# Weight sums of the second projection, made in the first layer and kept in DRAM, with another order of small steps in its blocks

## The chip, the cores and the metric

The kernel runs on one core of a Trainium2 chip. The core has five engines that each follow their own list of instructions: PE (TensorE, matrix products), DVE (VectorE), ACT (ScalarE), POOL (GpSimd) and SP (SyncE, which only issues DMAs here). An engine works through its list in order, and an instruction whose semaphore wait is not met holds up everything behind it on that engine. POOL issues DMAs too, out of the same list as its arithmetic.

The metric is the device time of one execution in microseconds, lower being better. Before the change it was 1901.19 us, the median of three runs (1899.56 to 1901.35).

## The reference, cut to what matters

Two layers, each an attention block and a gated block, all on x of 2048 rows by 448 features. The weights are the same in both layers.

```python
def _A_ref(x, wqkv, wo):              # D = 448, 16 heads of 28
    qkv = (x @ wqkv).reshape(B, S, 3, H, Dh) ...
    p = _softmax(einsum(q, k) * Dh ** -0.5)
    return (p @ v) @ wo
def _B_ref(x, w_gate, w_up, w_down):  # F = 1792
    return (_sigmoid(x @ w_gate) * (x @ w_up)) @ w_down
x = A_x
x = x + _A_ref(_layernorm(x), ...)
x = x + _B_ref(_layernorm(x), ...)
x = x + _A_ref(_layernorm(x), ...)
x = x + _B_ref(_layernorm(x), ...)
```

## The kernel before, in words

The rows of x are worked in four blocks of 512 (`b0` to `b3`), and x stays in SBUF. The program is a straight list: no scheduler moves anything, so the order of the calls in the Python source is the order on each engine. Small steps are threaded into the larger ones by hand, through lists of functions (`fill`, `points`, `between`).

**First layer's projection** (start to about 118 us). For each block, `qk` makes seven 128-column tiles of Q and K on PE (`qkp`, L618). ACT copies a tile out as float16 (L865), DVE makes the remainder (L866, the "low" part), ACT squares (L868) and DVE takes maxima (L872) that PE sums into `qnorm` and `knorm` (L844, L847), three tiles late. `vals` makes V (`vp`, L643 to L645), which ACT copies out (L1114). A block's normalised rows come from `norm` (DVE statistics; POOL `rs`, L333 and L335), `squares` (DVE scaling L362 and 32x32 transposes L379 into a tile `xs`), `store` (four DMAs of SP, `xs` to the DRAM tile `xt_scr`, L391) and `gather` (SP reads `xt_scr` back, L399 and L401). Beside it `Measure.read` loads weights whose sizes are wanted later; the rows of gate and up weights are loaded by POOL (six DMAs, L215 and L218, tile `raw`).

**The test of the bounds.** During the V of the third block DVE writes `guard`, `worst` and `flag` (L1216 to L1225). Every engine then loads `flag` into a register (L1231) and branches (L1232) over a part that is needed only for loose bounds. In the program this stands behind two of the four V products of the last block, and the other two stand behind the place where the branches meet.

**The gated block** ends with a tail: the last products with the down weights (`dnp`, L1875) in pieces, whose banks DVE adds into x (L1893). Down weights come by POOL's queue (`dn`, L1769). Beside the tail the second layer's projection is prepared: `add_pair(0)`, `(1)` and `(2)` make the sums of pairs of Q/K weight tiles from the raw weights, which POOL loads (`read_pairs`, L728 to L731): four additions on DVE (L254), four high parts on ACT (L263), six low parts on DVE (L266), and for the third pair two scalings ahead (L747). `load_rest` loads what is left of the weights (six DMAs of SP, L760 to L763). Block 2 of x is normalised there too: statistics, POOL's `rs` and `off` (L333 to L346), `lift` on ACT (L350), transposes (L358).

**Second layer's projection** (about 957 to 1061 us). `qk_sums` works blocks 0, 2 and 3 with the weight sums, by seven products of halves in place of eight: `chain` and `side` products (L633), whose results ACT and DVE add (L962, L978) into tiles `one` and `two`; a single tile `alone` (L1004) has no partner. `points`, `fill` and the list `before` say where steps of other blocks stand among these.

SBUF tiles come from 19 equal slots. `put` returns a slot to the end of the free list, `put_next` to its front, so that the next `get` takes it; a tile in a reused slot waits until everything that used the slot is done.

Of the kernel before, what the change touches and what calls it, by code (L numbers as in the profile page):

```python
# [121 lines left out]
def interleaved_layers(ctx: ExitStack, tc: tile.TileContext, x_in, wqkv, wo, w_gate, w_up,  # L122
# [181 lines left out]
    class Block:  # L304
# [79 lines left out]
        def store(self, queues=(nc.sync,)):  # L384
            xs = self.xs
            uid[0] += 1
            self.scr = dpool.tile([NQ, 32, 4, P], F32, name=f"xt_scr{uid[0]}", tag="xt_scr",
                                  bufs=2)
            for i in range(4):
                r = slice(32 * i, 32 * i + 32)  # L390
                queues[i % len(queues)].dma_start(  # L391
                    self.scr[:, :, i, :].rearrange("j r n -> r j n"),
                    xs[r].rearrange("r j t c -> r j (t c)"))
            big.put(xs)
# [255 lines left out]
    o_parts = dpool.tile([P, 2, 4, D], F16, name="o_parts")  # L650
    gu_parts = dpool.tile([NP, 2, P, N_SUMS, P], F16, name="gu_parts")
    dn_parts = dpool.tile([N_DN, P, NP, 2, DN], F16, name="dn_parts")

    class WeightsQKV:
        def tiles(self):
# [80 lines left out]
        def load(self):  # L736
            self.held, self.sums = [], []

        def add_pair(self, j):
            v, t = self.pair(j), big.get("wsums", [P, 32, P], F16)  # L740
            self.held.append(t)
            self.sums.append(t[:, 0:N_SUMS])
            m = [int(i > ALONE) for i in PAIRS_QK[j]]
            by = up[:, m[0]:m[0] + 1]
            if m[0] != m[1]:
                for z in range(2):
                    nc.vector.tensor_scalar(v[:, :, z], v[:, :, z], up[:, m[z]:m[z] + 1], None,  # L747
                                            op0=ALU.mult)
# [71 lines left out]
    def project(layer, wq, begun):  # L820
# [69 lines left out]
        def qk_sums(b, blk, points, before=None, defer=False):  # L890
# [132 lines left out]
            if before:  # L1023
                before(False)
            pa.c11_c22()
# [6 lines left out]
            pb.c21()  # L1032
            pb.tiles[0].low(pb.one)
            pa.c12()
            pb.c12()
            if before:
                before()
# [12 lines left out]
            pc.third()  # L1050
            at(4)
            pb.tiles[0].square()
            pc.c11_c22()
# [11 lines left out]
            squares = deque([lone.square, pc.tiles[0].square, pc.tiles[1].square])  # L1065
            if not defer:
                squares.popleft()()
            pc.tiles[1].high()
            pc.tiles[1].low(pc.two)
            while squares and not defer:  # L1070
                squares.popleft()()
            at(5)

            def finish(whole=True):
                if not whole:
                    squares.popleft()()
                    return
# [85 lines left out]
        if layer == 0:  # L1163
# [3 lines left out]
                    lambda: b2.ready(0, 1), lambda: (b2.ready(2, 3), b3.store())]  # L1167
            fin = qk(1, b1, fill, None)
            vals(1, b1, {0: b3.gather, 2: fin})
            add = tell.add  # L1170
            fin = qk(2, b2, [idle, lambda: b3.ready(0, 1), lambda: b3.ready(2, 3), idle, add,
                             add, add], None)
            fin = qk(3, blks[3], [add, add, add], fin)
        else:
# [5 lines left out]
            fin = qk_sums(0, blks[0], {0: ready[0:1] + s3[0:1], 1: ready[1:2], 2: s3[1:2],  # L1180
                                       4: ready[2:3], 5: ready[3:4]})
            vals(0, blks[0], {0: both(s3[2], s3[3], s3[6]), 1: both(fin, s3[4], s3[7]),
                              2: both(s3[5], s3[8], s3[9], b3.store),
                              3: both(h2[0], h2[1], b3.gather)})
            fin = qk(1, b1, h2[2:9], None)
            big.put(*wq.qk)
            vals(1, b1, {0: h2[9], 1: both(fin, *h3[0:2]), 2: both(*h3[2:4]),
                         3: both(*h3[4:6])}, banks=(3, 0, 2, 1))
            fin = qk_sums(2, b2, {0: h3[6:7], 1: h3[7:8], 2: h3[8:9], 4: h3[9:10]}, None, True)
# [14 lines left out]

        def guard_of_norms():
# [7 lines left out]
            guard = big.get("guard", [H, S], F16)  # L1213
            zero = big.get("zero", [H, S], F16)
            nc.gpsimd.memset(zero, 0.0)
# [3 lines left out]
            big.put(guard, zero)  # L1219

# [9 lines left out]
        vals(3, blks[3], {}, range(2))  # L1230
# [551 lines left out]
    def gated(layer, first, wt, wq):  # L1782
# [243 lines left out]
        for b, p in seq:  # L2026
# [58 lines left out]
            if b == NB - 1 and not last and p == NP - 2:  # L2085
                wq.read_pairs((0, 1))
# [157 lines left out]
```

## Time and profile before

| | |
|---|---|
| time, median of three runs | 1901.19 us |
| time of the profiled execution | 1900.52 us |
| its span, first instruction to last | 1898.8 us |
| PE busy | 1880.8 us, 99% of the span |
| DVE busy | 1478.7 us, 78% |
| ACT busy | 1425.2 us, 75% |
| POOL busy | 249.2 us, 13% |

A row of a timeline gives the start and the length in us, the engine, the line of the kernel, the operation, the tiles written and read, and in brackets how long the engine was idle ahead of it and what ended that. A row of the waits gives who waited for what, the total, the count and the longest, in us. A row of the windows gives for a stretch of time the busy time and count of each engine, then the clock granted to PE, the busy share of the DMA engines and GB/s.

### The profile page before, as it was taken

The numbers are of one execution on the slowest core, as the hardware profiler recorded it, in microseconds if no ns is written. First come the engines' busy times: TensorE is split into PE (matmuls) and PEld (weight loads), VectorE is DVE, ScalarE is ACT, GpSimd is POOL, SyncE is SP. The second block draws the span as 40 slices with busy tenths as digits, with TensorE's granted clock in tenths as the row PEclk, the third lists the DMA queues.
The fourth block names the chain that finished last, engine by engine and source line by source line (L and its number), as shares of the span: only waits on it lengthen the run. The fifth ranks groups of instructions, "written<-read, shape, count | busy, mean of one in ns | idle before, by whom it ended". The sixth has DMA issues, their size and how long they took to land. (4 is left out here: it accounts for less than half of the span.)

```text
span 1898.8 us, 57166 instructions
## 1 busy us (share of the span) xinstructions
PE 1880.8 (99%) x24531; PEld 1385.4 (73%) x24531; DVE 1478.7 (78%) x2984; ACT 1425.2 (75%) x1885; POOL 249.2 (13%) x482
## 2 busy tenths in 40 slices
PE   9999999999999999999999999999999999999999
PEld 4456656656566899999967556678766768999999
DVE  7758989898977887788876577787787688877664
ACT  5569999999993655555567799999999746555541
POOL 3023112222102111112310000000000021111110
PEclk9999999999999999999999999999999999999999
DMA  7675444344323755646672421222120256566553
GB/s 247 192 216 159 134 131 121 111 121 132 102 87 100 256 206 203 241 183 225 220 192 85 107 51 32 47 52 48 31 52 13 75 159 225 200 228 225 211 207 141
DMA packets 116471, 273.78 MB, mean 144 GB/s; under 512 B 14478, under 2 KB 72590, under 8 KB 116080
## 3 DMA queue, kind: packets, MB, share of 16 engines
q0 software_dynamic: 33120, 163.33, 24.0%
q1 hardware_dynamic: 81936, 105.33, 19.9%
q8 instruction: 194, 3.18, 0.7%
q10 hardware_dynamic: 1152, 1.38, 0.3%
q14 instruction: 69, 0.57, 0.1%
HBM read 210.98 MB, written 50.62 MB: 138 GB/s over the span
## 5 line engine op out<-in xcount | busy, mean ns | idle before, releaser
L1530 ACT ACTIVATE prob_s<-sc 128x1536 f32<-128x1536 f32 (+1 forms) x657 | 888.3, 1478 | 9.6 <-PE sc L1515 8.0
L1566 PE MATMUL acc<-prob_s,val_s 128*32 128x256 f32 (+3 forms) x7700 | 580.3, 384 | 0.9 <-issue 0.9
L1515 PE MATMUL sc<-qp_s 114*32 114x512 f16 x7868 | 562.8, 379 | 0.8 <-DMA qp_s<-g_scr 0.8
L633 PEld LDWEIGHTS <-gu_s 128*128 128x128 f16 x4368 | 426.7, 98 | 46.4 <-PE op L1695 0.7
L1515 PEld LDWEIGHTS <-qp_s 114*32 114x32 f16 x8192 | 293.1, 96 | 186.7 <-issue 72.4
L1566 PEld LDWEIGHTS acc<-prob_s,val_s 128*32 128x32 f32 x7700 | 295.4, 110 | 122.6 <-issue 12.5
L1875 PE MATMUL dnp<-dn_s,hparts_s 128*128 128x224 f16 x2184 | 246.0, 259 | 1.7 <-DVE x L1893 1.7
L633 PE MATMUL chain<-xwide_s,gu_s 128*128 128x256 f16 x2016 | 247.5, 273 | 0.1
L1875 PEld LDWEIGHTS <-hparts_s 128*128 128x128 f16 x2184 | 210.2, 98 | 7.0 <-issue 1.9
L1546 DVE SCALAR_TENSOR_TENSOR power_q<-power_q,expo_q 128x512 f32<-128x512 f32 x243 | 168.2, 692 | 8.3
L1948 ACT COPY one_q<-chain 128x256 f32<-128x256 f32 x224 | 82.4, 372 | 113.2 <-PE chain L633 112.7
L1964 DVE TENSOR_TENSOR one_q<-side,one_q 128x512 f32<-128x512 f32 x112 | 72.1, 686 | 95.7 <-PE side L633 95.4
L633 PE MATMUL side<-xshort_s,gu_s 128*128 128x256 f16 x1120 | 140.6, 273 | 0.0
L1756 POOL DMA_DIRECT2D gu_s<-gu_parts x104 | 56.3, 541 | 428.2 <-PE side L633 426.8
L1595 DVE STREAM_TRANSPOSE oturned_q<-acc 128x512 f32<-128x512 f32 x32 | 22.9, 717 | 98.9 <-PE acc L1566 98.8
L1828 ACT CAST hparts_s<-hsums_q 128x256 f16<-128x256 f32 (+1 forms) x152 | 71.5, 485 | 37.9 <-DVE hsums_q L1840 23.4
L1566 PE MATMUL acc<-power_q,val_s 128*32 128x256 f32 (+3 forms) x300 | 94.2, 396 | 0.0
L633 PE MATMUL side<-xwide_s,gu_s 128*128 128x256 f16 x672 | 91.7, 273 | 0.0
L618 PE MATMUL qkp<-xhl_s,wqk_s 128*128 128x512 f16 x385 | 86.5, 379 | 0.9 <-ACT wqk_s L235 0.6
L1975 ACT ACTIVATE one_q<-one_q 128x512 f32<-128x512 f32 x56 | 35.3, 630 | 64.3 <-DVE one_q L1964 64.0
L1540 DVE TENSOR_SCALAR expo_q<-aside,base 128x512 f32<-128x512 f32 x81 | 60.6, 748 | 22.7 <-PE aside L1515 22.4
L1832 DVE TENSOR_TENSOR hparts_s<-hsums_q,hparts_s 128x256 f16<-128x256 f32 (+1 forms) x152 | 72.7, 520 | 5.8 <-ACT hparts_s L1828 5.8
(261 smaller groups left out, 2396.7 us busy)
## 6 DMA issues: line engine op xcount, KB each, us to landing
gu_s<-gu_parts POOLq DMA_DIRECT2D x104, 800.0 KB, 6.0
dn_s<-dn_parts POOLq DMA_DIRECT2D x42, 784.0 KB, 7.3
qp_s<-qk_scr SPq DMA_DIRECT2D x96, 224.0 KB
gu_parts<-pack_s POOLq DMA_DIRECT2D x14, 800.0 KB, 3.8
xt_scr<-xs_s SPq DMA_DIRECT2D x48, 224.0 KB
xraw_s<-xt_scr SPq DMA_DIRECT2D x12, 768.0 KB
qk_scr<-qkhl_q SPq DMA_DIRECT2D x35, 256.0 KB
qp_s<-qk_scr SPq DMA_DIRECT2D x64, 112.0 KB
```

The lines of the kernel that those rows point to most:

```text
L618: nc.tensor.matmul(pm, w, x, start=(i == 0), stop=(i == len(terms) - 1))
L633: nc.tensor.matmul(pm, a, x, start=(first and i == 0), stop=(i == len(terms) - 1), skip_group_check=True)
L1515: nc.tensor.matmul(ps[32 * j:32 * j + 32, :], hd.k[:, keys], hd.q[:, qb * W:(qb + 1) * W], start=True, stop=True, tile_position=(0, 32 * j))
L1530: nc.scalar.activation(prob[:, 0:n, :], ps[:, 0:n, :], AF.Exp, scale=exp_scale)
L1540: nc.vector.tensor_scalar(y, ps, base2[:, 0:1], -126.0, op0=ALU.mult, op1=ALU.max)
L1546: nc.vector.scalar_tensor_tensor(p, p, c[k], y, op0=ALU.add, op1=ALU.mult)
L1566: nc.tensor.matmul(acc[qb * VC:(qb + 1) * VC, s], v[:, kc % TB, h, :], probs[c * NB + qb][:, s], start=(kc == 0 and a == 0), stop=(kc == N ...
L1828: nc.scalar.copy(to[:, :, 0], a)
L1832: nc.vector.tensor_tensor(to[:, :, 1], a, to[:, :, 0], op=ALU.subtract)
L1875: nc.tensor.matmul(pm, a[:, x, t], w[:, p, y], start=(begin and n == 0 and (j == 0 or alone)), stop=(n == 2), skip_group_check=True)
L1948: nc.scalar.copy(to, pm)
L1964: nc.vector.tensor_tensor(one[m], side[m], one[m], op=ALU.add)
```

## The change

- **Sums kept.** `add_pair` becomes `keep_pair`: the same arithmetic, but it writes a tile `pack`, and POOL stores that to a new DRAM tile `qs_parts` (three pieces of 800 KB). It runs in the first layer's projection: pair 0 in the third block's `qk`, pair 1 behind `guard`, pair 2 at the head of the last block's V. At the end of the first layer's gated block SP loads the three pieces (`wq.load(0)` to `(2)`).
- **The tail of the gated block.** With the three `add_pair` gone, all of block 2's normalisation and its `store` stand at once ahead of the additions into x, two `load_dn` stand there in place of three (the loop issues the rest), and `load_rest` is called there.
- **Order inside `qk_sums`.** The addition of `c11_c22` of the third pair and a square stand ahead of the point 4; the last high and low part of the third pair join the deferred steps; the earlier block's deferred steps are taken up in other places, and its last ones ahead of `pb`'s low part. The half steps of blocks 2 and 3 are spread anew.
- **`store` returns `xs` by `put_next`.** The next `get` takes that slot. In the first layer's projection, for block 2, this is the `raw` tile of the gate and up rows.
- **`zero`** is set ahead of the power that `guard` needs.

```diff
@@ store
-            big.put(xs)
+            big.put_next(xs)
@@ WeightsQKV
-        def add_pair(self, j):
-            v, t = self.pair(j), big.get("wsums", [P, 32, P], F16)
-            self.held.append(t)
-            self.sums.append(t[:, 0:N_SUMS])
+        def keep_pair(self, j):
+            v, t = self.pair(j), big.get("pack", [P, N_SUMS, P], F16)
...
             split_sums(t, v, by)
+            nc.gpsimd.dma_start(qs_parts[j], t)
+            big.put(t)
...
+        def load(self, j):
+            self.held.append(big.get("wsums", [P, 32, P], F16))
+            self.sums.append(self.held[j][:, 0:N_SUMS])
+            nc.sync.dma_start(self.sums[j], qs_parts[j])
@@ qk_sums
             pc.third()
+            pc.c11_c22()
+            pb.tiles[0].square()
             at(4)
-            pb.tiles[0].square()
-            pc.c11_c22()
...
-            squares = deque([lone.square, pc.tiles[0].square, pc.tiles[1].square])
-            if not defer:
-                squares.popleft()()
-            pc.tiles[1].high()
-            pc.tiles[1].low(pc.two)
-            while squares and not defer:
-                squares.popleft()()
+            def last_parts():
+                pc.tiles[1].high()
+                pc.tiles[1].low(pc.two)
+            todo = deque([lone.square, last_parts, pc.tiles[0].square, pc.tiles[1].square])
+            while todo and not defer:
+                todo.popleft()()
@@ project, layer 0
+            fill[4] = lambda: wq.read_pairs((0,))
             fin = qk(1, b1, fill, None)
             vals(1, b1, {0: b3.gather, 2: fin})
-            fin = qk(2, b2, [idle, lambda: b3.ready(0, 1), lambda: b3.ready(2, 3), idle, add,
-                             add, add], None)
+            fin = qk(2, b2, [lambda: wq.keep_pair(0), lambda: b3.ready(0, 1),
+                             lambda: (b3.ready(2, 3), wq.read_pairs((1, 2))), idle, add, add,
+                             add], None)
...
             big.put(guard, zero)
+            if layer == 0:
+                wq.keep_pair(1)
...
-        vals(3, blks[3], {}, range(2))
+        vals(3, blks[3], {} if layer else {0: lambda: wq.keep_pair(2)}, range(2))
@@ gated, the tail
-            wq.load()
-            for _ in range(3):
+            for _ in range(2):
                 wt.load_dn(nc.gpsimd)
-            wq.add_pair(0)
-            wq.add_pair(1)
+            wq.load(1)
+            wq.load(2)
+            wq.load_rest()
             third = after[2]
-            turns = third.squared()
-            between = deque([turns[0:1], [lambda: wq.read_pairs((2,))] + turns[1:2],
-                             turns[2:5] + turns[6:8], turns[5:6] + turns[8:] + [third.store],
-                             [third.gather, lambda: wq.add_pair(2)],
-                             [wq.load_rest, wq.load_values]])
+            for do in third.squared() + [third.store]:
+                do()
+            between = deque([[], [], [third.gather, wq.load_values], [], [], []])
```

Three places show what moves. On POOL, in the first layer's projection, beside the second block's Q and K: the loads of the gate and up rows stand ahead of `rs` of the fourth block. The brackets name the semaphores that a row waits for (DMAHW are the queues that SP and ACT issue into, by number). Before:

```order
41 L215 DMA raw_s_555<-in_B_w_gate_dram 128x3x256 [waits DMAHW1_49,DMAHW2_49,DMAHW0_49,Activation_49]
42 L218 DMA raw_s_555<-in_B_w_gate_dram 64x256 x2
43 L215 DMA raw_s_555<-in_B_w_up_dram 128x3x256
44 L218 DMA raw_s_555<-in_B_w_up_dram 64x256 x2
45 L333 TENSOR_SCALAR rs_607<-mv_606 128x4 [waits DVE_49]
46 L335 TENSOR_TENSOR rs_607<-rs_607,nhalf 128x4 [waits Pool_49]
```

After:

```order
41 L215 DMA raw_s_556<-in_B_w_gate_dram 128x3x256 [waits DMAHW5_49,DMAHW6_49,DMAHW4_49,DMAHW7_49,DMAHW0_49,DVE_49]
42 L218 DMA raw_s_556<-in_B_w_gate_dram 64x256 x2
43 L215 DMA raw_s_556<-in_B_w_up_dram 128x3x256
44 L218 DMA raw_s_556<-in_B_w_up_dram 64x256 x2
45 L333 TENSOR_SCALAR rs_608<-mv_607 128x4 [waits DVE_49]
46 L335 TENSOR_TENSOR rs_608<-rs_608,nhalf 128x4 [waits Pool_49]
47 L732 DMA raws_s_692<-in_A_wqkv_dram 128x3x128 [waits DMASW0_49,Activation_49]
48 L734 DMA raws_s_692<-in_A_wqkv_dram 64x128 [waits DMASW1_49]
```

The order of the rows is the same; the first load now waits for the third block's last transpose (DVE) and its four stores (DMAHW4 to 7), whose slot it takes, and no longer for the use of raw Q/K/V weights on ACT.

On DVE, ahead of the branch of the first layer, before (`guard`, `worst` and `flag`, then the load of the flag):

```order
166 L1210 SCALAR_TENSOR_TENSOR bnd_1126<-top_1125 16x1
167 L1216 TENSOR_SCALAR guard_s_1155<-zero_s_1156,bnd_1126 16x2048
168 L1224 TENSOR_REDUCE worst_1128<-bounds_1200 1x1
169 L1225 TENSOR_SCALAR flag_1127<-worst_1128,back 1x1
170 L1231 TENSOR_LOAD flag_1127
171 L1232 COMPARE_AND_BRANCH
```

After, from the row right behind the one that writes the flag (pair 1's ten rows stand between `guard` and `worst` in the same way):

```order
190 L746 TENSOR_SCALAR raws_s_899<-raws_s_899,up 128x4x128 x2
191 L254 TENSOR_TENSOR sums_q_1275<-raws_s_899 128x256
192 L254 TENSOR_TENSOR sums_q_1275<-sums_q_1275,raws_s_899 128x256
193 L254 TENSOR_TENSOR sums_q_1276<-raws_s_899 128x256
194 L254 TENSOR_TENSOR sums_q_1276<-raws_s_899,sums_q_1275 128x256
195 L266 SCALAR_TENSOR_TENSOR pack_s_1272<-raws_s_899,ones,pack_s_1272 128x256
196 L266 SCALAR_TENSOR_TENSOR pack_s_1272<-sums_q_1275,ones,pack_s_1272 128x512
197 L266 SCALAR_TENSOR_TENSOR pack_s_1272<-sums_q_1276,ones,pack_s_1272 128x384
198 L266 SCALAR_TENSOR_TENSOR pack_s_1272<-raws_s_899,ones,pack_s_1272 128x256
199 L266 SCALAR_TENSOR_TENSOR pack_s_1272<-sums_q_1276,ones,pack_s_1272 64x128
200 L266 SCALAR_TENSOR_TENSOR pack_s_1272<-raws_s_899,ones,pack_s_1272 64x256
201 L1244 TENSOR_LOAD flag_1163
```

Twelve instructions of pair 2 now stand between the writing of the flag and DVE's load of it.

On DVE, in the tail of the first layer's gated block (`hparts` are parts of the hidden values, `x<-dnp` the additions into x, `sums` and `wsums` the weight sums). Before:

```order
2796 L1832 TENSOR_TENSOR hparts_s_13729<-two_q_18251,hparts_s_13729 128x256
2797 L1893 SCALAR_TENSOR_TENSOR x<-dnp_17156,back,x 128x2x224
2798 L254 TENSOR_TENSOR sums_q_18437<-raws_s_18234 128x256
2799 L254 TENSOR_TENSOR sums_q_18437<-sums_q_18437,raws_s_18234 128x256
2800 L254 TENSOR_TENSOR sums_q_18438<-raws_s_18234 128x256
2801 L254 TENSOR_TENSOR sums_q_18438<-raws_s_18234,sums_q_18437 128x256
2802 L266 SCALAR_TENSOR_TENSOR wsums_s_18436<-raws_s_18234,up,wsums_s_18436 128x256
2803 L266 SCALAR_TENSOR_TENSOR wsums_s_18436<-sums_q_18437,up,wsums_s_18436 128x512
```

After:

```order
2830 L330 BN_AGGR mv_18509<-st_0_18511 128x2
2831 L329 BN_STATS st_1_18514<-x 128x6
2832 L330 BN_AGGR mv_18509<-st_1_18514 128x2
2833 L329 BN_STATS st_2_18522<-x 128x6
2834 L330 BN_AGGR mv_18509<-st_2_18522 128x2
2835 L329 BN_STATS st_3_18525<-x 128x6
2836 L330 BN_AGGR mv_18509<-st_3_18525 128x2
2837 L358 STREAM_TRANSPOSE xs_s_18540<-lifted_q_18532 128x14x32
2838 L358 STREAM_TRANSPOSE xs_s_18540<-lifted_q_18534 128x14x32
2839 L358 STREAM_TRANSPOSE xs_s_18540<-lifted_q_18536 128x14x32
2840 L358 STREAM_TRANSPOSE xs_s_18540<-lifted_q_18538 128x14x32
2841 L1906 SCALAR_TENSOR_TENSOR x<-dnp_18550,back,x 128x2x224
```

Ahead of the first addition of the tail stand four statistics and four transposes in place of twenty instructions of two pairs of weight sums.

More of the change, by code (lines that the diff above doesn't have):

```diff
@@ L654, in interleaved_layers, with __init__ @@
     class WeightsQKV:
+        def __init__(self):
+            self.held, self.sums = [], []
         def tiles(self):
@@ L1024, in qk_sums @@
                 before(False)
+                before(False)
             pa.c11_c22()
@@ L1032, in qk_sums @@
             pb.c21()
+            if before:
+                before()
             pb.tiles[0].low(pb.one)
@@ L1203, in project @@
         worst = cpool.tile([1, 1], F32, name=f"worst{layer}", tag="worst", bufs=1)
+        guard = big.get("guard", [H, S], F16)
+        zero = big.get("zero", [H, S], F16)
+        nc.gpsimd.memset(zero, 0.0)
         def guard_of_norms():
@@ L2085, in gated @@
             if b == NB - 1 and not last and p == NP - 2:
-                wq.read_pairs((0, 1))
+                wq.load(0)
         b = NB - 1
```

26 lines of the change are left out of this document (10 added, 16 removed).

## The prediction

> **What bounds the kernel now.** The page first, then who waits on PE.
>
> ```profile
> PE 1880.8 (99%) x24531; PEld 1385.4 (73%) x24531; DVE 1478.7 (78%) x2984; ACT 1425.2 (75%) x1885; POOL 249.2 (13%) x482
> ```
>
> PE works for all but 18 us of a span of 1898.8, and the change takes no product away. So time can only come out of PE's idle spots, and goes in by new ones. The view of the waits, for PE alone, lists those near the change:
>
> ```profile
> PE alone L1004 <- DMA wsums_s<-qk_parts: 2.1, 2, 1.7
> PE dnp L1875 <- DVE x L1893: 1.7, 1, 1.7
> PE chain L633 <- DVE x L1893: 1.6, 1, 1.6
> ...
> PE side L633 <- DVE one_q L978: 1.0, 2, 0.5
> ...
> PE vp L643 <- DVEq L1232: 0.9, 1, 0.9
> PE alone L1004 <- DVE peaks L1080: 0.9, 1, 0.9
> ...
> PE side L633 <- ACT val_s L1114: 0.7, 1, 0.7
> ...
> PE chain L633 <- ACT one_q L962: 0.4, 1, 0.4
> ```
>
> All but the row with DVEq stand in the first layer's tail and the second layer's projection. Together they are 8.4 us. A stall costs somewhat more than its idle time, as the one at the branch shows in PE's timeline:
>
> ```profile
> 115.27 0.35 PE L641 MATMUL vp<-wv_s,xhl_s 128*128 128x448 f16 x1
> 116.55 0.36 PE L643 MATMUL vp<-wv_s,xhl_s 128*128 128x448 f16 x1 [0.92 <-DVEq L1232]
> 116.75 0.35 PE L644 MATMUL vp<-wv_s,xhl_s 128*128 128x448 f16 x1
> ```
>
> From start to start these products take 0.20 us, but 1.28 across the stall: 1.08 lost where 0.92 is idle. I add 0.16 for each stall.
>
> **The gains, one by one.** The tail, on DVE, PE, ACT and SP:
>
> ```profile
> 930.49 0.68 DVE L1893 SCALAR_TENSOR_TENSOR x<-dnp,back,x 128x448 f32<-128x448 f32 x1
> ...
> 940.47 16.26 PE L1875 MATMUL dnp<-dn_s,hparts_s 128*128 128x224 f16 x168 [1.74 <-DVE x L1893]
> ...
> 951.22 0.87 DVE L747 TENSOR_SCALAR raws_s<-raws_s,up 128x512 f32<-128x512 f32 x2
> ...
> 954.34 0.71 ACT L263 ACTIVATE wsums_s<-raws_s,ones 128x512 f16<-128x512 f32 x1
> ...
> 955.95 0.47 DVE L266 SCALAR_TENSOR_TENSOR wsums_s<-raws_s,ones,wsums_s 64x256 f16<-64x256 f32 x1
> 956.45 1.83 DVE L1893 SCALAR_TENSOR_TENSOR x<-dnp,back,x 128x448 f32<-128x448 f32 x3
> 958.33 1.47 PE L633 MATMUL chain<-xwide_s,wsums_s 128*128 128x256 f16 x12 [1.61 <-DVE x L1893]
> 959.70 0.80 SPq L760 DMA_DIRECT2D wsums_s<-qk_parts  x1
> ```
>
> - At 940.47 PE waits for an addition into x that stood behind two pairs of sums on DVE. Now four statistics, the POOL and ACT steps and four transposes stand there, which I put at some 7 us from 931.1 (statistics 2.9, POOL 1.6 behind them, two ACT steps of 0.7, a transpose of 0.65: their lengths further on in the tail); with the addition that is about 938.6, near where PE runs dry (940.47 less 1.9). Gain 1.6 of at most 1.9; none if the ACT steps come later than I think.
> - At 958.33 the additions stood behind pair 2, 951.22 to 956.42. That is gone: 1.7.
> - The loads of the lone tile's weights start at 959.70. They now start about 20 us earlier, ahead of the last products of the tail: 2.1 + 0.32 for two stalls = 2.4.
> - Order in the blocks: the additions that PE awaited go ahead of the other steps. One_q on DVE 1.0 + 0.32, one_q on ACT 0.4 + 0.16, the maxima before `alone` 0.9 + 0.16: 2.9. Of the stall by ACT's `val` I take half of 0.9, as the half steps are only spread otherwise: 0.4.
>
> Sum 9.0, between 7 (the first or the `val` stall stays) and 9.9 (all go). The two last loads of down weights are issued later:
>
> ```profile
> dn_s<-dn_parts POOLq DMA_DIRECT2D x42, 784.0 KB, 7.3
> ```
>
> They go out when the tail's first two pieces are done, at about 937.6 and 938.2, and are wanted at about 947 and 951 by PE's pace of 0.097 us (16.26 us for 168): 9.4 us for 7.3. I price them at 0.1, at most 3 beside the 1.6 MB of sums loaded at the same time.
>
> **Where it costs: the first layer's V and `store`.** Pair 0's ten DVE steps stand where DVE now idles for several us in the third block, and I cost them at nothing; without that cover they would hold a bank of PE. The two other places do cost. First `put_next`:
>
> ```profile
> 45.54 0.77 POOL L215 DMA_DIRECT2D raw_s<-in_B_w_gate_dram  x1
> ...
> 53.97 0.19 POOL L333 TENSOR_SCALAR rs<-mv 128x4 f32<-128x4 f32 x1 [4.65 <-DVE mv L330]
> ...
> 49.40 3.25 SPq L391 DMA_DIRECT2D xt_scr<-xs_s  x4
> 57.27 0.38 SPq L399 DMA_DIRECT2D xraw_s<-xt_scr  x1
> ...
> 55.30 0.51 DVE L362 TENSOR_SCALAR xn_s<-x,mv,rs 128x448 f32<-128x448 f32 x1 [0.65 <-POOL rs L335]
> 58.07 0.27 DVE L872 TENSOR_TENSOR sq_q<-sq_q 128x256 bf16<-128x256 bf16 x1
> ...
> 58.85 0.27 PE L844 MATMUL qnorm<-sq_q,ind 128*128 128x256 bf16 x1
> ...
> raw_s<-in_B_w_gate_dram POOLq DMA_DIRECT2D x1, 384.0 KB, 7.4
> ...
> 54.00:56.40 2.40, 2.40 (x14) 1.10 (x12) 1.72 (x4) 1.23 (x2) 1.19 (x2) 1.00 1.02 307
> 56.80:58.00 1.20, 1.20 (x8) 0.50 (x6) 1.17 (x3) 1.00 (x2) 0.00 (x0) 1.00 0.07 26
> ```
>
> The gate and up loads, issued from 45.54, must now wait for the four stores of `xs`, issued 49.40 to 52.65. Those landed just before SP's gather at 57.27. In the windows the DMA engines are full until 56.4 and empty behind; with the gate and up rows out of the way (384 KB each and a third as much again for their short last parts: 1 MB, some 3 us at 307 GB/s), the stores should land about 54.5 (not before 53.5, since the last is issued until 52.65; not after 57.2). Six issues of POOL take 3.8 us (45.54 to 49.3). So `rs`, at 53.97 before, comes at 58.4 instead, and DVE's scaling 1.33 later at 59.7 in place of 55.30. DVE works in order, so the low part and maximum behind it, done at 58.35 before, come 4.4 later at 62.8. PE wants that maximum at 58.85: a stall of **4.0** (bounds 3.0 and 6.7). Nothing behind it needs to wait again, as DVE and ACT are by then ahead of PE.
>
> Second the branch:
>
> ```profile
> 108.21 0.74 DVE L1216 TENSOR_SCALAR guard_s<-zero_s,bnd 16x2048 f16<-16x2048 f16 x1 [2.41 <-POOL zero_s L1215]
> 111.39 0.16 DVE L1224 TENSOR_REDUCE worst<-bounds 1x1 f32<-1x16 f32 x1 [2.44 <-PE bounds L1223]
> 111.59 0.20 DVE L1225 TENSOR_SCALAR flag<-worst,back 1x1 int32<-1x1 f32 x1
> ...
> 115.66 0.54 ACT L1114 ACTIVATE val_s<-vp 128x448 f32<-128x448 f32 x1 [1.54 <-PE vp L641]
> ...
> L1232 DVEq EVENT_SEMAPHORE  x2: 21/21/21, 116.5 to 1059.5; - x2
> ...
> L1231 DVEq TENSOR_LOAD <-flag x2: 528/536/544, 111.8 to 1055.0; - x2
> ...
> L1231 ACTq TENSOR_LOAD <-flag x2: 287/288/288, 115.7 to 1058.7; - x2
> ```
>
> Pair 1 fits: `guard` need not wait for `zero` any more, and the two idle times of 2.4 take its ten steps. Pair 2 does not. DVE loads the flag at 111.8 and passes the join at 116.5, 4.7 later (4.5 in the second layer), and PE starts right behind. Now pair 2 stands ahead of the load. In the tail its last ACT part ended at 955.05, 3.8 after its start, and its last DVE part started 4.7 after it. ACT's row of the load, at 115.7 while its copy ran until 116.20, shows that an engine's queue takes instructions ahead of the arithmetic; so the load goes out when the last wait is met, after 3.8, plus 0.2 for what pair 1 delays. Join at 120.5 in place of 116.5: **4.0** (3.8 to 4.9).
>
> **PE's clock.** Both stalls make PE idle for 4 to 5 us, which it never is before. What happens then only the ends of the trace show:
>
> ```profile
> 1.25 5.64 PE L302 MATMUL still<-still_q 128*128 128x512 f16 x13 [1.25 <-DVE warm L184]
> ...
> 1897.70:1898.80 1.10, 0.00 (x0) 0.00 (x0) 0.00 (x0) 0.00 (x0) 0.00 (x0) 0.50 0.00 0
> ```
>
> At the start the products of 128x512 take 0.43 us for 5.6 us, twice their later length, and at the very end, with PE done, the granted clock reads 0.50. Idle of 1.9 us (at 940.47) leaves no trace. So a stall of 4 us likely halves the clock for some time: nothing at best, 2.8 us (half of 5.6) at worst. I take 1.5 for each, in the middle: 3.0. The Trainium skill (TensorE: Matmul & The Clock Gate, What's actually happening) gives free-running windows of about 3.4 us, back to half speed after an idle one and to full speed after a busy one; by that, as an estimate, a stall costs up to 1.7 more. The trace agrees on the halves; how long they last inside a kernel no run here shows yet.
>
> **Sum.** -9.0 + 0.1 + 4.0 + 4.0 + 3.0 = +2.1 on the profiled 1900.5, which is 0.7 under the median of the runs. On the median: **1903 us**. About 0.2% (3.8 us) is what a measurement can tell from no change, so this is no change.
>
> **Rivals.**
> - *The stores land as late as before (slower).* If what fills the DMA engines until 56.4 is not the gate and up rows, the loads start at 57.2, PE stalls for 6.7 and the clock loses more: +2.7 and +1, about 1907. It decides from a landing at 56.2 on. For it: the stores are issued late in that stretch themselves. Against it: the 1 MB that leaves. 0.16.
> - *The clock stays halved for as long as at the start (slower).* 2.8 twice: +2.6, about 1905.6. By the page's rule a busy window ends it, against that stands the start of this trace. 0.14. The late down weights (at most +3, 1906) get 0.06.
> - *The branch costs nothing more (faster).* If most of the 4.7 us from load to join is a fetch that is already under way by the time of DVE's load, the join stays near 117 and PE waits hardly more than now: -4.0 and -1.5, about 1897. For it: SP and POOL branch quickly in the first layer. Against it: both of DVE's are alike. 0.14.
> - *`put_next` costs nothing* (POOL's loads find the stores landed before 50.5, which SP's issues exclude, or other gains): -5.5, about 1897. 0.06.
>
> My forecast keeps 0.44. Faster 0.20, same 0.44, slower 0.36. The range takes in the rivals' times and a little of their mixtures: 1896.5 to 1908.5.
>
> **What will show it.** In the changed profile: PE idle ahead of `qnorm` near 58.9 for about 4 us, released by DVE's maximum, with POOL's six loads behind 54; PE idle near 119 (115.3 plus the shift) for about 5, released by DVEq; products of 448 columns at 0.38 instead of 0.19 behind each; no wait on x, on the DMA of `alone` or on one_q from 938 to 1040. Wrong I would be most by a clock that does not drop (-3.0), or by a gain in the tail that turns into a wait for ACT's lifted rows or for down weights.

## The result, and the profile after

| | before | after |
|---|---|---|
| median of 10 runs each, us | 1900.86 (1899.12 to 1901.48) | 1905.64 (1903.53 to 1906.48) |
| ratio after / before, 95% interval | | 1.0026 [1.0016, 1.0036] |
| the profiled execution: its time, its span, us | 1900.5, 1898.8 | 1905.42, 1903.7 |
| mean granted TensorE clock | 1.000 | 0.996 |

The changed kernel is slower by 0.26%, about 5 us; the interval reaches from 0.16%, just inside the 0.2% that the prediction counts as no change, to 0.36%. The forecast was 1903. Products and weight loads are as many as before, and the page's line of busy time and the view of the waits, for PE alone, show the trade:

```profile
PE 1883.9 (99%) x24531; PEld 1391.4 (73%) x24531; DVE 1478.4 (78%) x2984; ACT 1425.1 (75%) x1885; POOL 250.2 (13%) x485
```

```profile
PE qnorm L850 <- DVE sq_q L878: 5.8, 1, 5.8
PE vp L643 <- DVEq L1245: 4.6, 1, 4.6
...
PE side L633 <- ACT val_s L1122: 0.9, 1, 0.9
...
PE side L633 <- DVE one_q L984: 0.4, 1, 0.4
...
PE dnp L1888 <- DVE x L1906: 0.2, 1, 0.2
```

The stalls of the tail and of the second layer's projection have shrunk from 8.4 us to under 2; two new ones, both in the first layer's V, take 9.5 us more (5.8, and 4.6 where 0.9 was). PE is also *busy* 3.1 us longer with the same number of products: some of them ran slower.

Since PE does the same products in both kernels, and all but some forty of 24531 in the same order, the place of each loss and gain can be read by setting the starts of the same product side by side:

| the product | before | after | difference |
|---|---|---|---|
| `qkp` ahead of the first stall | 57.99 | 57.84 | -0.15 |
| `qnorm` L844 / L850, the first stall's end | 58.85 | 64.64 | +5.8 |
| a product of `vp` behind it | 61.15 | 68.89 | +7.7 |
| last product ahead of the branch, `vp` L641 | 115.27 | 122.97 | +7.7 |
| first product behind the branch, `vp` L643 | 116.55 | 127.90 | +11.35 |
| last products of V behind the branch | 121.10 | 135.14 | +14.0 |
| the gated block's end, `dnp` | 930.03 | 943.75 | +13.7 |
| first layer's last piece, `dnp` x168 | 940.47 | 952.63 | +12.2 |
| second layer's first `chain` | 958.33 | 968.73 | +10.4 |
| behind the lone tile's weights, `chain` | 975.02 | 983.03 | +8.0 |
| last V product ahead of the second layer's first scores | 1060.54 | 1066.45 | +5.9 |
| second layer's first scores | 1062.12 | 1067.52 | +5.4 |
| `dnp` near the end | 1895.10 | 1900.14 | +5.05 |

So 7.9 are lost at the first stall and 6.3 at the branch, and 7.8 are won back in the tail and the second projection. The rest is 1.3 of small drifts. 0.5 of them is a wait of the second layer's first scores for a DMA, 0.8 before and 0.3 after; it is 0.2 in a kernel of the experiments whose second layer is that of before, so it can't be counted as a gain of the change.

**The first stall.** These are rows of the timelines of SP, POOL, DVE and PE after (start, length, engine, line, operation; in brackets the idle time ahead and what ended it), those that the prediction named:

```profile
49.09 2.99 SPq L391 DMA_DIRECT2D xt_scr<-xs_s  x4
...
55.95 0.38 SPq L399 DMA_DIRECT2D xraw_s<-xt_scr  x1
```

```profile
56.47 0.77 POOL L215 DMA_DIRECT2D raw_s<-in_B_w_gate_dram  x1 [11.08 <-DMA xt_scr<-xs_s]
...
60.21 0.19 POOL L333 TENSOR_SCALAR rs<-mv 128x4 f32<-128x4 f32 x1
```

```profile
61.55 0.51 DVE L362 TENSOR_SCALAR xn_s<-x,mv,rs 128x448 f32<-128x448 f32 x1 [7.20 <-POOL rs L335]
...
64.31 0.27 DVE L878 TENSOR_TENSOR sq_q<-sq_q 128x256 bf16<-128x256 bf16 x1
```

```profile
64.64 0.37 PE L850 MATMUL qnorm<-sq_q,ind 128*128 128x256 bf16 x1 [5.77 <-DVE sq_q L878]
...
65.02 0.58 PE L643 MATMUL vp<-wv_s,xhl_s 128*128 128x448 f16 x1
65.39 0.58 PE L644 MATMUL vp<-wv_s,xhl_s 128*128 128x448 f16 x1
```

POOL stands idle for 11.08 us, until the stores of `xs` have landed, and only then issues its first gate load. The two steps of `rs` stand behind its six loads, DVE's scaling behind `rs`, the maximum behind the scaling, and PE's `qnorm` behind the maximum: four engines in a row, each merely keeping its order. And the products of 448 columns behind the stall start 0.37 us apart where they took 0.19.

**The clock.** The windows of after (us of the window, then busy time and number of instructions of PE, PEld, DVE, ACT and POOL, the granted clock, the DMA engines' busy share, GB/s):

```profile
61.00:62.00 1.00, 0.00 (x0) 0.00 (x0) 0.45 (x1) 0.80 (x2) 1.00 (x2) 0.91 0.93 287
62.00:63.00 1.00, 0.00 (x0) 0.00 (x0) 0.96 (x3) 0.83 (x2) 0.85 (x2) 0.50 1.04 377
...
68.00:69.00 1.00, 1.00 (x5) 0.49 (x4) 1.00 (x3) 0.00 (x0) 0.00 (x0) 0.68 0.27 92
...
126.00:127.00 1.00, 0.00 (x0) 0.00 (x0) 0.00 (x0) 0.00 (x0) 0.08 (x1) 0.84 0.95 272
...
133.00:134.00 1.00, 1.00 (x20) 0.37 (x12) 0.00 (x0) 0.30 (x1) 0.00 (x0) 0.75 0.94 250
```

A clock of 0.91 in one microsecond is full for 0.82 of it and half for the rest. So it fell at 61.82 and rose at 68.64, and fell again at 126.68 and rose at 133.50: 6.82 us both times. In the first stretch PE worked from 64.64 on, 4.0 us at half speed, which costs about 2.0 (the table has 7.7 - 5.8 = 1.9); in the second from 127.90 on, 5.6 us, which costs about 2.8 (the table has 14.0 - 11.35 = 2.7).

**The branch.** DVE and PE after, and the rows of the flag's load and of DVE's join, grouped by line (number, shortest, median and longest ns, first and last start):

```profile
119.39 0.20 DVE L1238 TENSOR_SCALAR flag<-worst,back 1x1 int32<-1x1 f32 x1
119.52 0.86 DVE L746 TENSOR_SCALAR raws_s<-raws_s,up 128x512 f32<-128x512 f32 x2
...
124.23 0.47 DVE L266 SCALAR_TENSOR_TENSOR pack_s<-raws_s,ones,pack_s 64x256 f16<-64x256 f32 x1
```

```profile
122.63 0.71 ACT L263 ACTIVATE pack_s<-raws_s,ones 128x512 f16<-128x512 f32 x1
```

```profile
L1244 DVEq TENSOR_LOAD <-flag x2: 536/540/544, 123.4 to 1060.9; - x2
```

```profile
L1245 DVEq EVENT_SEMAPHORE  x2: 21/21/21, 127.8 to 1064.7; - x2
```

```profile
127.90 0.56 PE L643 MATMUL vp<-wv_s,xhl_s 128*128 128x448 f16 x1 [4.57 <-DVEq L1245]
```

DVE writes the flag at 119.39, but loads it only at 123.4, when the last ACT part of pair 2 has ended (122.63 + 0.71), and not after DVE's own last part, which starts only at 124.23: the load runs ahead of DVE's arithmetic and behind the last wait that stands before it. From load to join it takes 4.4 us, and PE starts right behind. POOL loads the flag later still, 1.9 us behind DVE, here and in two of the kernels below; the join then follows DVE's load by 4.2 to 5.3 us, in the other seven kernels of this document by 3.7 to 5.2, so POOL's late load is not what the join waits for. The Trainium skill (Perfetto Trace Analysis, DVE / Act Engine Instruction) has the sequencer push such an instruction into a wait queue and go on to the next one; the trace agrees, with the load 0.8 us ahead of a low part that stands before it.

**The tail.** PE after:

```profile
952.63 16.26 PE L1888 MATMUL dnp<-dn_s,hparts_s 128*128 128x224 f16 x168 [0.19 <-DVE x L1906]
968.73 1.52 PE L633 MATMUL chain<-xwide_s,wsums_s 128*128 128x256 f16 x12
```

PE's stalls of 1.74 and 1.61 are down to 0.19 and nothing, and no wait on the lone tile's weights is left. Of the stalls in the projection, that by ACT's `val` stays, with 0.9.

### The profile page after: what moved, and what is told of

Its sections match the earlier page's. It is cut to its first block, busy times and chain, and to the rows that moved or that the text cites. A ratio compares the mean times of both kernels' runs of the same rounds, so it can differ in the third digit from the quotient of the medians.

```text
span 1903.7 us, 57169 instructions
## 1 busy us (share of the span) xinstructions
PE 1883.9 (99%) x24531; PEld 1391.4 (73%) x24531; DVE 1478.4 (78%) x2984; ACT 1425.1 (75%) x1885; POOL 250.2 (13%) x485
## 5 line engine op out<-in xcount | busy, mean ns | idle before, releaser
L1579 PEld LDWEIGHTS acc<-prob_s,val_s 128*32 128x32 f32 x7700 | 300.1, 110 | 115.0 <-issue 10.7
```

The costliest lines, as they stand in the source:

```text
L1579: nc.tensor.matmul(acc[qb * VC:(qb + 1) * VC, s], v[:, kc % TB, h, :], probs[c * NB + qb][:, s], start=(kc == 0 and a == 0), stop=(kc == N ...
```

## The experiments

The theory after the result: the one call of `put_next` makes the first stall, pair 2 ahead of the flag's load makes the second, each of the two halves the clock because PE is idle, and the rest of the change is a gain of some 8 us that these three hide. The rivals: the first stall needs the new DVE work of pair 0 as well; the clock falls by something other than idleness; the branch costs what it costs wherever pair 2 stands. Each kernel was measured beside the kernel before on its chip; times are medians.

### Pairs kept, `put_next` undone

```diff
-        def store(self, queues=(nc.sync,)):
+        def store(self, queues=(nc.sync,), back=False):
...
-            big.put_next(xs)
+            (big.put if back else big.put_next)(xs)
...
-                            3: lambda: (b2.squares(), b2.store(), tell.read())}
+                            3: lambda: (b2.squares(), b2.store(back=True), tell.read())}
```

> The changed kernel with one line undone: block 2's store in the first layer's projection gives xs back at the end of the free list. My theory (POOL's gate and up loads wait for the four stores, and rs of block 3 stands behind them): PE's 5.8 us wait ahead of qnorm near 58.9 us and the halved clock behind it go, 7.8 us in all by the shift of PE's products, so about 1897.8 us, 3 under the kernel before. The rival (the slots that move with put_next collide in several places, or the stores land late for another reason): the wait stays or moves, and the time stays above 1903.

Measured: 1896.12 us against 1899.52, ratio 0.9983 [0.9974, 0.9992]. By the ratios this is 8.2 us better than the changed kernel, where the expectation had 7.8. The wait of `qnorm` is gone, and only the branch is left of the two:

```profile
PE vp L643 <- DVEq L1245: 4.4, 1, 4.4
```

Pair 0 and all other steps still stand where they stood, so they are not what PE waited for. Behind the branch the clock here was half for one stretch of 3.4 us (120.16 to 123.57), not two.

### The kernel before, with `put_next` alone

```diff
-        def store(self, queues=(nc.sync,)):
+        def store(self, queues=(nc.sync,), front=False):
...
-            big.put(xs)
+            (big.put_next if front else big.put)(xs)
...
-                            3: lambda: (b2.squares(), b2.store(), tell.read())}
+                            3: lambda: (b2.squares(), b2.store(front=True), tell.read())}
```

> The kernel before with only that line changed: block 2's store in the first layer returns xs to the front. My theory: 7.8 us more than before, about 1908.7 us, with a wait of about 5.8 us ahead of qnorm and half speed behind it for one or two windows of 3.4 us. The rival (it needs the kept sums beside it, through POOL's added loads or DMA traffic): within 1 us of 1900.9.

Measured: 1906.17 against 1899.52, ratio 1.0034 [1.0021, 1.0048].

```profile
PE qnorm L844 <- DVE sq_q L872: 5.8, 1, 5.8
```

The same stall of 5.8, and by the starts of the same products +7.7 at 61, +6.9 behind the branch and +5.2 at the end. The branch's own wait takes part of the loss up (0.15 is left of 0.92), which is why the time is 6.5 above the kernel before by the ratio and not the 7.8 expected. One line in the kernel before thus makes it slower by as much as the whole change does. Both ways round, the first stall is settled: it is `put_next`, and it needs nothing else.

### PE kept busy in both stalls

Products that nobody reads, of tiles that lie ready, go into a spare bank: 26 ahead of `qnorm`, 20 ahead of the branch. The kernel thus does 46 products more.

```diff
+    def idle_products(blk, i, n):
+        pm = bank(i, "idle")
+        for k in range(n):
+            nc.tensor.matmul(pm, blk.hi[:, 0, 0:P], blk.hi[:, 1, :], start=(k == 0),
+                             stop=(k == n - 1))
...
+                if layer == 0 and b == 1 and i == 6:
+                    idle_products(blk, 4, 26)
...
+        if layer == 0:
+            idle_products(blks[3], 6, 20)
         loose = nc.values_load(flag[0:1, 0:1], min_val=0, max_val=1)
```

> The changed kernel with products that nobody reads put into PE's two waits: 26 of 128x512 ahead of the waiting qnorm (5.6 us at full clock) and 20 ahead of the branch (4.3 us). If PE's idleness halves its clock, both waits stay as long but the products behind them run at full speed: 1.8 + 2.5 us less, about 1901.3 us. If the clock falls for another reason (the load on the chip, the branch), the added products run at half speed and the time rises, to 1908 or more; if half speed costs nothing, 1905.6.

Measured: 1900.83 against 1899.52, ratio 1.0007 [0.9997, 1.0016]: 3.6 us less than the changed kernel by the ratios of the medians, 5.0 by the spans of the two profiles (1898.7 against 1903.7). The mean clock is 1.000. The waits are still there, only filled; what is gone is the half clock behind them. So idleness of PE lowers the clock. By the starts of the same products PE stands 3.1 us better behind the two places than in the changed kernel; the products put in cost 1.5 of their own there (a new wait of 0.3 behind the first, a join 5.3 us behind the flag's load in place of 4.4), so the half clock costs the 4.6 of the table, of the 14 us lost. The other 1.9 between the two profiles lie in the attention and behind it, where nothing was changed.

### Pair 2 behind the branch

```diff
-        vals(3, blks[3], {} if layer else {0: lambda: wq.keep_pair(2)}, range(2))
+        vals(3, blks[3], {}, range(2))
...
         vals(3, blks[3], {}, [2], 0 if layer == 0 else 7)
+        if layer == 0:
+            wq.keep_pair(2)
```

> The changed kernel with pair 2's sums moved behind the branch, right after the copies of the last V tile that stands there. My theory (only its place ahead of DVE's load of the flag costs): PE's wait at the branch is back at about 1 us and the clock stays, 6.3 us less, to which come 0 to 3 us because DVE's powers and four more ACT copies stand in the first attention tiles: 1899.3 to 1902.3 us. The rival (5 us of DVE work cost PE that much wherever they stand): about 1905.

Measured: 1904.13 against 1899.52, ratio 1.0023 [1.0014, 1.0032]. The branch's wait falls from 4.6 to 1.5, and the same products start 5.9 us earlier at 135 than in the changed kernel. By 138, 4.8 of it is gone again. The waits of PE, and rows of ACT and of PE behind the branch:

```profile
PE sc L1530 <- ACT prob_s L1545: 3.1, 1, 3.1
PE vp L643 <- DVEq L1245: 1.5, 1, 1.5
...
PE vp L1104 <- DMA wv_s<-v_parts: 1.0, 1, 1.0
```

```profile
130.64 0.71 ACT L263 ACTIVATE pack_s<-raws_s,ones 128x512 f16<-128x512 f32 x1
131.25 2.77 ACT L1545 ACTIVATE prob_s<-sc 128x1536 f32<-128x1536 f32 x2
```

```profile
132.73 1.47 PE L1530 MATMUL sc<-qp_s 114*32 114x512 f16 x12 [3.14 <-ACT prob_s L1545]
134.14 0.55 PE L643 MATMUL vp<-wv_s,xhl_s 128*128 128x448 f16 x1
134.48 0.58 PE L644 MATMUL vp<-wv_s,xhl_s 128*128 128x448 f16 x1
```

The expectation was too good, and in time the other outcome on record came nearer, 1905: pair 2 costs about as much here as ahead of the flag, but in another way. Pair 2's ACT parts now stand ahead of the attention's first exponentials, PE waits for these, and the clock falls again, as the spacing of 0.34 at 134 shows, where it is 0.20 at full clock. What the branch costs does depend on pair 2, 1.5 against 4.6 (that rival falls), but behind it ACT is the engine that has no room.

### Both pairs one place earlier

Pair 1 goes into the last block's Q and K, and pair 2 to where pair 1 stood, between `guard` and `worst`.

```diff
-            fin = qk(3, blks[3], [add, add, add], fin)
+            fin = qk(3, blks[3], [add, add, add, idle, lambda: wq.keep_pair(1)], fin)
...
-                wq.keep_pair(1)
+                wq.keep_pair(2)
...
-        vals(3, blks[3], {} if layer else {0: lambda: wq.keep_pair(2)}, range(2))
+        vals(3, blks[3], {}, range(2))
```

> The changed kernel with nothing but the places of two pairs moved: pair 1 behind the fifth tile of the last block's Q and K, pair 2 where pair 1 stood, between guard and worst, so that nothing stands between the flag and DVE's load of it. My theory: the two gaps of DVE there do not quite hold pair 2, the flag comes about 1.2 us later than before the change, PE's wait at the branch falls from 4.6 to about 2 us, too short for the clock to fall: 5 us less than the changed kernel, about 1899.5 us beside 1904.3 on this chip. The rival (any place on DVE in this stage costs PE the 5 us): no gain, 1904.

Measured: 1903.79 against 1901.09, ratio 1.0016 [1.0007, 1.0025], some 2 us better than the changed kernel where more was expected. The branch's wait halves, to 2.3; but pair 1 now delays the last block's maxima (`knorm` waits 0.7 and everything behind is 1.0 later by 113), a wait of 1.1 for `wv_s` in the second layer is new, and the clock falls all the same:

```profile
124.58 0.35 PE L641 MATMUL vp<-wv_s,xhl_s 128*128 128x448 f16 x1
127.23 0.56 PE L643 MATMUL vp<-wv_s,xhl_s 128*128 128x448 f16 x1 [2.30 <-DVEq L1245]
```

```profile
126.00:127.00 1.00, 0.00 (x0) 0.00 (x0) 0.00 (x0) 0.00 (x0) 1.00 (x3) 1.00 0.72 228
127.00:128.00 1.00, 0.77 (x3) 0.33 (x4) 0.00 (x0) 0.00 (x0) 1.00 (x2) 0.59 0.85 184
...
130.00:131.00 1.00, 1.00 (x5) 0.26 (x2) 0.00 (x0) 0.00 (x0) 0.57 (x2) 0.71 0.96 205
```

An idle time of only 2.3 us was enough for one stretch at half speed, from 127.2 to 130.6.

### The same with `put_next` undone

The edits of the first and of the last experiment together.

> The same moves and block 2's xs given back to the end of the list. If the two costs are apart from each other, they add up: 7.8 and 5 us less than the changed kernel, about 1891.5 us, 8 under the kernel before (ratio 0.996). If one hides the other, about 1896, as with xs alone.

Measured: 1897.44 against 1901.09, ratio 0.9985 [0.9976, 0.9994], which is no better than the first experiment and misses what was expected, a ratio of 0.996, by some 5 us. It is the time of the other outcome on record (one cost hides the other), but the rows show a new cost instead: the earlier place of pair 1 costs more when there is no first stall ahead of it. That DVE then has had no time to get ahead of PE is argued, not shown.

```profile
106.59 0.27 PE L853 MATMUL knorm<-sq_q,ind 128*128 128x256 bf16 x1 [1.65 <-DVE sq_q L878]
107.39 0.27 PE L853 MATMUL knorm<-sq_q,ind 128*128 128x256 bf16 x1 [0.53 <-DVE sq_q L878]
107.50 0.41 PE L643 MATMUL vp<-wv_s,xhl_s 128*128 128x448 f16 x1
107.70 0.58 PE L644 MATMUL vp<-wv_s,xhl_s 128*128 128x448 f16 x1
```

Two waits of together 2.2 us at `knorm` and a stretch at half clock behind them (spacing 0.37 from 107.70) cost 4.2, where the branch's wait shrinks to 1.2.

### The kernel before, with the new order in the blocks alone

No pair is kept and no weights move: the order of additions, squares and half steps in the second layer's projection alone.

```diff
             pb.c21()
+            if before:
+                before()
             pb.tiles[0].low(pb.one)
...
             pb.c12()
-            if before:
-                before()
...
-            at(4)
-            pb.tiles[0].square()
             pc.c11_c22()
+            pb.tiles[0].square()
+            at(4)
...
-            vals(1, b1, {0: h2[9], 1: both(fin, *h3[0:2]), 2: both(*h3[2:4]),
-                         3: both(*h3[4:6])}, banks=(3, 0, 2, 1))
+            vals(1, b1, {0: h3[0], 1: both(h3[1], h3[2], fin), 2: both(*h3[3:5]),
+                         3: both(*h3[5:7])}, banks=(3, 0, 2, 1))
```

> The kernel before with only the order inside the second layer's blocks changed (additions, squares, half steps), and no sums kept. My theory: from the changed kernel's shifts behind 971 us on, 0.7 us for the first block, 1.2 and 0.7 for the later ones, 0.5 at the end, less 0.4 of new waits: about 2.7 us less than before, 1896.8 beside 1899.5. The rival (these gains came only because the tail was done earlier): within 1 us of before.

Measured: 1897.86 against 1901.09, ratio 0.9988 [0.9979, 0.9997]: 2.3 us faster, close to what was expected. In the waits of PE those by `one_q` and by the maxima are gone, those of the tail are all there, and one has grown:

```profile
PE alone L1004 <- DMA wsums_s<-qk_parts: 2.2, 2, 1.8
PE dnp L1877 <- DVE x L1895: 1.7, 1, 1.7
PE side L633 <- ACT val_s L1116: 1.7, 1, 1.7
PE chain L633 <- DVE x L1895: 1.6, 1, 1.6
```

In the first layer, where this kernel is the kernel before, two waits of 0.6 stand that the profile before lacks, and PE is 0.7 later from 70 to 115: so much comes and goes between executions of the same code.

### All three pairs earlier, `put_next` undone

From the misses: DVE has room in the second block's last V tile and the third block's first Q and K tile, ACT has none behind the branch, and the last block's Q and K have none at all. So pairs 0 and 2 are read together and kept there, and pair 1 alone stays between `guard` and `worst`.

```diff
-            big.put_next(xs)
+            (big.put if back else big.put_next)(xs)
...
-            fill[4] = lambda: wq.read_pairs((0,))
+            fill[4] = lambda: wq.read_pairs((0, 2))
...
-            vals(1, b1, {0: b3.gather, 2: fin})
+            vals(1, b1, {0: b3.gather, 2: fin, 3: lambda: wq.keep_pair(0)})
...
-            fin = qk(2, b2, [lambda: wq.keep_pair(0), lambda: b3.ready(0, 1),
-                             lambda: (b3.ready(2, 3), wq.read_pairs((1, 2))), idle, add, add,
+            fin = qk(2, b2, [lambda: wq.keep_pair(2), lambda: b3.ready(0, 1),
+                             lambda: (b3.ready(2, 3), wq.read_pairs((1,))), idle, add, add,
...
-        vals(3, blks[3], {} if layer else {0: lambda: wq.keep_pair(2)}, range(2))
+        vals(3, blks[3], {}, range(2))
```

> Both causes taken away: block 2's xs given back to the end, pairs 0 and 2 read together and made earlier (pair 0 behind the last V tile of block 1, pair 2 behind the first Q/K tile of block 2, where DVE idles), pair 1 alone between guard and worst, nothing between the flag and its load. My theory: no new wait of PE is left in the first layer and the gain of the tail stays whole: 8.3 us less than before, ratio about 0.9957; up to 2 us of it may go to PE's maxima of block 2, which have 0.7 us to spare. The rival (the first layer's projection has no room for the 14 us of DVE work on its path, wherever it stands): a new wait of some us appears, ratio 0.998 or more, as with both moved before.

Measured: 1894.03 against 1900.53, ratio 0.9967 [0.9955, 0.9979]: 6.3 us faster than before, and by the ratios 0.6% faster than the changed kernel. The mean clock is 1.000. Expected were some 2 us more. Against the kernel before, waits of `qnorm` cost 1.4 in the first layer, and the branch 0.6 more, since load to join took 5.2 there in place of 4.6; drifts in the attention give 1.4 of this back. In the second layer's projection a wait for `wv_s` costs 0.9. PE's waits at these places:

```profile
PE vp L643 <- DVEq L1246: 1.5, 1, 1.5
...
PE qnorm L851 <- DVE sq_q L879: 0.8, 2, 0.4
PE vp L1105 <- DMA wv_s<-v_parts: 0.7, 1, 0.7
```

Against the kernel before the same products are 2.4 us later behind the branch, 1.0 later at the end of the first layer, and 6.1 earlier at the end. With the two long stalls gone the gains of the change are there to see, and they were in the changed kernel all the time.

## Why the prediction was right, and by how much it was off

The forecast held every larger loss and gain in its place and with its sign; the sum came out 3 us too low, and that is the difference between "no change" (0.44) and "slower" (0.36). By its own terms:

| term | forecast, us | measured, us |
|---|---|---|
| tail, first stall | -1.6 | -1.55 |
| tail, second stall | -1.7 | -1.77 |
| loads of the lone tile's weights | -2.4 | -2.43 |
| order in the blocks, and `val` | -2.9 - 0.4 | -2.1 |
| late down weights | +0.1 | 0 |
| `put_next` | +4.0 (3.0 to 6.7) | +5.9 |
| the branch | +4.0 (3.8 to 4.9) | +3.6 |
| the clock | +3.0 (0 to 5.6) | +1.9 + 2.7 |
| small drifts, in the attention and at the second layer's first scores | 0 | -1.3 |
| sum | +2.1 | +5.05 |

- **The gains.** The three of the tail came out within 0.1 us. In the blocks 1.2 is missing (the down weights give 0.1 of it back): the half expected of the `val` stall did not come (0.9 is left where 0.7 was), and DVE's `one_q` keeps 0.4. The new order alone gave 2.3 by the ratio.
- **`put_next`, +5.9 where the forecast took 4.0: the mis-sized term.** The chain is the one described, POOL's six loads, `rs`, the scaling, the low part, the maximum, `qnorm`. What failed is the step "with the gate and up rows out of the way (...), the stores should land about 54.5". They landed at 55.95 (SP's gather starts then), and POOL went on at 56.47, half a microsecond behind SP. The forecast divided the bytes taken away by 307 GB/s, the rate from 54 to 56.4, when POOL's loads were nearly done and the stores themselves were under way; and it let the stores take as long without those loads as behind them. By the DMA records of the two traces their 512-byte pieces move from 52.2 to 56.9 before and from 49.9 to 55.6 after: they start 2.3 us earlier and take 5.7 us in place of 4.7. The windows of after, with those loads gone:

```profile
44.00:50.00 6.00, 6.00 (x30) 2.70 (x29) 5.22 (x11) 3.34 (x6) 1.40 (x2) 1.00 0.87 315
50.00:54.00 4.00, 4.00 (x21) 1.92 (x20) 3.86 (x11) 1.63 (x4) 0.00 (x0) 1.00 0.98 205
```

And one of before, when its stores are under way:

```profile
54.00:55.00 1.00, 1.00 (x7) 0.49 (x5) 0.66 (x2) 0.88 (x2) 0.92 (x2) 1.00 1.14 333
```

After the change the DMA engines were still full from 50 to 54, at two thirds of the forecast's rate, with little but the stores under way. So the landing came 1.3 us earlier where 2.7 were forecast, POOL went on behind the 56.2 from which the first rival decides, and the stall came nearer to its 6.7 than to 4.0. The rival's own reason (something else fills the engines until 56.4) is not quite this one; its sign "the stores are issued late in that stretch themselves" was the right one. Why the same stores move more slowly without the loads ahead of them, no run tells.
- **The branch, +3.6.** Right in place and mechanism, and in size within 0.4: load when the last ACT part is done, join 4.4 later. The rival that most of it is a fetch already under way falls. Why load to join takes so long, 3.7 to 5.3 us in the first layer of these kernels, no run tells.
- **The clock, +4.6 where the forecast took 3.0.** It took the middle between nothing and the start's 5.6 us of half speed, and the second rival had the upper end. Measured are 6.82 us of half clock, of which PE worked 4.0 and 5.6. That idleness is the cause was argued in the forecast, and the busy products show it. The Trainium skill's free-running windows of 3.4 us (TensorE: Matmul & The Clock Gate, What's actually happening) fit what is seen: 6.82 is twice 3.41, and the two falls, at 61.82 and 126.68, lie 64.86 us apart, 19 times 3.41. But by its rule a window must be idle; here the window ahead of the fall in the kernel with both pairs earlier (123.8 to 127.2, if windows are so long) had PE at work until 124.9, a third of it. For the way back 2.2 us of work in the window from 126.68 to 130.09 were too little, and half clock lasted on through the next; in the kernel before with `put_next` alone 2.65 us from 64.53 to 67.94 were enough, and the clock rose there. The start of the trace, which the second rival set against a busy window's ending the half clock, is no sign against it: from 1.25 to 6.7 PE worked longer than one such window. The forecast's estimate of 1.7 a stall by the Trainium skill was too low by up to 1.0.
- **Pair 0 at nothing** was right: with `put_next` undone no wait of PE stands at it.

The two terms that were too small, by 1.9 and 1.6, and gains short by 1.1, less 0.4 at the branch and drifts of 1.3, make the 3 us. The drifts stood in no term; that they made the miss smaller is luck.

## What to carry to other kernels

A buffer handed to the next taker early, or a transfer's issue put behind another transfer on an engine that also computes, delays all the arithmetic behind it on that engine; follow the order of each engine to the one that bounds, as here POOL, DVE, PE. When a load is taken out of a full stretch of DMA, don't divide bytes by the stretch's rate: what remains may fill the engines at a lower one. And price a stall of TensorE over two microseconds with a stretch at half clock behind it; work that must go somewhere is best put where each engine that it uses has idle time, all of them, and a change that nets nothing may hold a gain that two misplaced lines hide.

## What the runs showed of the hardware beyond what was expected

- **The clock falls after less idle time than the forecast took for it.** 1.7 us idle (before, at 940; the prediction's 1.9 holds its 0.16 beside) left it full; 2.3 us (pairs earlier) and two waits of 1.65 and 0.53 (the same with `put_next` undone) each gave a stretch of 3.4 us at half speed; the 5.8 and 4.6 of the changed kernel gave 6.8 each; but the same 5.8 in the kernel before with `put_next` alone, and a wait of 4.4 with `put_next` undone, gave only 3.4. How a stall lies against the windows thus matters as much as its length, so that the same stall has no one price: 1.3 to 2.7 us in these runs.
- **DMA engines as good as full have no one rate.** Busy at 0.98 they moved 205 GB/s with the stores of `xs` (50 to 54 after), 333, at 1.14, with the same stores in the kernel before (54 to 55), and 377 with loads (62 to 63 after). The stores' pieces have the same size both times, so their size alone does not set the rate; what does stays open.
- **DVE's load of the flag does not wait for DVE's own arithmetic**, only for the last wait that stands ahead of it: 123.4 against a low part that starts at 124.23. So it is the waits for ACT that cost here; that a step whose inputs lie ready would have cost the branch nothing follows from this, but no run shows it.
